# ScalarE takes some k and v norms, the pieces get a new order, and 35 one-column copies go into the lead

## The chip, the cores and the metric

The kernel runs on one core of one Trainium2 chip. The metric is device time in microseconds; a run counts from the start of the program on the device to its end. Five engines work side by side, each on its own queue in order: TensorE (PE in the profile; its weight loads are PEld), VectorE (DVE), ScalarE (ACT), GpSimd (POOL) and SyncE (SP). They wait for each other on semaphores. PSUM, where TensorE writes, has eight banks here, numbered 0 to 7.

## The reference

Eight batches, eight heads, 576 positions, head size 64, and 32 memory slots; then a feed-forward layer over all 4608 tokens.

```
a    = softmax(phi)                      # over the 32 slots of a head
k_m  = a^T k,  v_m = a^T v               # 32 x 64 for each head
attn = softmax(q k_m^T / 8) v_m
x    = attn, heads side by side          # 4608 x 512
h    = max(x w1, x w2, x w3)             # 4608 x 768
out  = h w_out                           # 4608 x 512
```

## The kernel before, in words

The kernel is a list of small steps (pieces), written out by hand as one string at its end. Each word of it is a piece, a number and a batch: `F8@1` is step 8 of kind F for batch 1. A `!` sets the flag `swap`, which moves the piece's element-wise work to the other engine. `issue` turns a word into instructions, and each engine runs its instructions in the order of the words. Nothing reorders them afterwards. A second string gives the PSUM bank of each piece in turn, so it changes with the order.

The kinds that matter here (lines are those of the kernel before):

- `L0` to `L3`, `J`, `H`, `h`, `Y`: loads of phi, k, v, q (or parts of them) and of the weights, issued by GpSimd (L93, L97, L112, L119, L126), with a cast to bf16 for all but phi. `r` packs k beside a column of ones (L105 on ScalarE with `!`, L107 on GpSimd without).
- `E`: exp of phi (L234, ScalarE). `B`: the sums of k, v and the ones over positions (L256, TensorE, 72 small matmuls; in batches 0 and 1 split into `B0` for k and ones and `B1` for v). `N`: the norm, by the reciprocal of the sum of ones (L276, VectorE), which scales v (L280) and k (L291). `K`: transposes of the result (L306) and their copy out of PSUM, `kvt`. Here too `N0`, `K0` are for k and `N1`, `K1` for v in batches 0 and 1.
- `Q`: q transposed on VectorE (L321), two halves. `S`: scores (L342, TensorE) and their exp on ScalarE (L351). `a`, `s`, `c`, `m`, `X`: transpose, sum, reciprocal, product and transpose back (L401 to L441; `m` on GpSimd, or VectorE with `!`). For batch 0 and half of batch 1 `M`, `R`, `X` do the sum by a matmul with ones and ln and exp on ScalarE.
- `D`: the batch's v sums folded into the weights (L453, TensorE) and copied out (L177 or L181): `D3` gives `wp3`, the others parts of `wp`. `V`: w1 and w2 less w3 (L218), once.
- `F`: the first layer (L504, TensorE), 12 steps for each batch: even ones end in a relu, odd ones in a max on VectorE (L517).
- `t`, `T`: the second layer (L663, L681, L690, L699) with its copy out, and the output's DMA (`g` sends a held output on ScalarE's queue). For batches 2 to 7 the second layer is done instead by seven block products `P0` to `P6` (L615) from sums and differences of blocks: `A` of the activations, `U` of the weights (L540; GpSimd or VectorE by the flag; A with `!` is GpSimd's, U with `!` VectorE's).
- `Z`: matmuls on zeros in the lead; `W`, `O`: w3 transposed, and its product with w_out.

Two k buffers (`ko`), three buffers of packed k and v (`kvr`) and two q buffers take turns, so that a load also waits for the last reader of its buffer.

Of the kernel before, what the change touches and what calls it, by code (L numbers as in the profile page):

```python
# [15 lines left out]
def kernel(  # L16
# [28 lines left out]
    const = ctx.enter_context(tc.tile_pool(name="const", bufs=1))  # L45
# [18 lines left out]
    K1 = NP * NC * KS  # L64
# [65 lines left out]
    warm = const.tile([P, BANK], BF16, name="warm")  # L130
# [7 lines left out]
    for i in range(P // M):  # L138
# [4 lines left out]
    banks = iter(  # L143
        "".join(
            """
            00232204420145545045026402642602460246016042045026402462046064206402640230462064
            20642064206247042074204620460240640420402620420462046240724074204242020460246024
            602345040606426064026406416424126464642460263454342
            """.split()
        )  # L150
    )
# [1 line left out]
    def one_bank():  # L153
        return psum[:, int(next(banks))]
# [58 lines left out]
    def w_diff(n, swap):  # L213

        c, end = [(0, BANK), (BANK, DF), (2 * BANK, 2 * DF), (DF, 2 * BANK)][n]
        while c < end:
            e = min(end, (c // DF + 1) * DF)
            (nc.gpsimd if swap else nc.vector).tensor_tensor(  # L218
                out=w12[:, :, c:e],
                in0=w12[:, :, c:e],  # L220
                in1=w_sb[:, :, 2, c % DF : c % DF + e - c],
                op=ALU.subtract,
            )
            c = e
# [41 lines left out]
                        tile_position=(HP * a, M * j),  # L266
                    )

    def att_kv_norm(b, part=None):

        s = st[b]
        kvp = s["kvp", part]
        if part != 1:
            rden = s["rden"] = work.tile([P, NG], FP32, name="rden")
            s["kvn"] = work.tile([P, 3, P], BF16, name="kvn")
            nc.vector.reciprocal(out=rden, in_=kvp[:, :, 0 if part == 0 else D])  # L276
        rden, kvn = s["rden"], s["kvn"]
        if part != 0:
            v0 = 0 if part == 1 else D + 1
            nc.vector.tensor_tensor(  # L280
                out=kvn[:, 0].rearrange("p (a d) -> p a d", a=NG),
                in0=kvp[:, :, v0 : v0 + D],
                in1=rden.unsqueeze(2).to_broadcast([P, NG, D]),
                op=ALU.mult,
            )
        if part == 1:
            return
        k0 = D if part == 0 else 0
        for g in range(NG):
            kn = kvn[:, 1:3, HP * g : HP * (g + 1)]  # L290
            nc.vector.tensor_scalar_mul(  # L291
                out=kn.rearrange("p h (t d) -> p h t d", t=2),
                in0=kvp[:, g, k0 : k0 + D]
                .rearrange("p (d h) -> p h d", h=2)
                .unsqueeze(2)
                .to_broadcast([P, 2, 2, R]),
                scalar1=rden[:, g : g + 1],
            )

    def att_kv_t(b, swap, part=None):  # L300
# [422 lines left out]
    def ffn2_last(b, c0):  # L723
# [18 lines left out]
        for i, (c, po) in enumerate(zip(cs, pos)):  # L742
# [13 lines left out]
            else:  # L756
                nc.scalar.copy(out=ot[:, c], in_=po)
                nc.scalar.dma_start(out=rows, in_=ot[:, c])

    def issue(b, n, swap):  # L760

        i = int(n[1:]) if len(n) > 1 else None
# [8 lines left out]
            "r": lambda: pack(b, swap),  # L771
            "E": lambda: [att_exp(b, h) for h in (halves if b == 0 else [slice(0, NP)])],
            "B": lambda: att_kv(b, i),
            "N": lambda: att_kv_norm(b, i),
            "K": lambda: att_kv_t(b, swap, i),
            "Q": lambda: att_q(b, i),
            "S": lambda: att_score(b),
# [84 lines left out]
```

## Time and profile before

| | us |
|---|---|
| runs, median of 3 | 161.03 (160.45 to 161.09) |
| the profiled execution's own time | 160.41 |
| its span | 158.6 |
| TensorE busy | 150.2 (95%) |
| VectorE, ScalarE, GpSimd busy | 118.4, 98.4, 105.1 |
| last TensorE piece ends | 155.6 |

The profile is of one execution. A busy time counts what an engine was seen to do, whoever waited for it; idle time of an engine with nothing due costs nothing. The chain of waits goes back from the last instruction to what released it, step by step; what is on it set the end. A row of the cost table reads: line, engine, operation, what it writes and reads, shapes, count, then busy us, the mean of one in ns, and the idle time just before with what ended it. A timeline row reads: start and length in us, engine, line, operation, and the idle time before it, if any, in brackets.

### The profile page before, as it was taken

What the parts mean: (1) busy time and instruction counts of PE and PEld (TensorE: products, weight loads), DVE (VectorE), ACT (ScalarE), POOL (GpSimd) and SP (SyncE); (2) the same over time, 40 slices, a digit from 0 to 9 for tenths busy, and PEclk for the clock granted to TensorE, in tenths of its full rate; (3) what the DMA queues carried; (4) which work ended last, traced back from release to release, by engine and by line L of the source; (5) the groups of instructions that cost most, each with busy time, mean ns of one, the idle gap of its engine ahead of it and who ended that gap; (6) DMA issues with size and microseconds to landing.
All of it is one profiled execution on the core that took longest, in us unless ns stands there. A gap on an engine that the chain in (4) does not pass through costs nothing.

```text
span 158.6 us, 5184 instructions
## 1 busy us (share of the span) xinstructions
PE 150.2 (95%) x2228; PEld 100.0 (63%) x2228; DVE 118.4 (75%) x205; ACT 98.4 (62%) x140; POOL 105.1 (66%) x100
## 2 busy tenths in 40 slices
PE   6996798999899999999999999999999999999992
PEld 2342544673456548646777577787874888888871
DVE  2032802789998997897998889899999868899851
ACT  4206335753787799997787789888976934124210
POOL 7960101993039959949969998999979996910000
PEclk9999999999999999999999999999999999999999
DMA  5999999999999999999999999999803500331544
GB/s 153 162 199 208 206 209 213 281 207 209 205 283 218 301 236 235 315 263 283 276 223 208 230 371 231 250 184 186 262 0 136 198 6 0 132 132 70 198 160 171
DMA packets 22934, 31.78 MB, mean 200 GB/s; under 512 B 1152, under 2 KB 18560, under 8 KB 22912
## 3 DMA queue, kind: packets, MB, share of 16 engines
q0 software_dynamic: 16128, 21.43, 71.3%
q1 hardware_dynamic: 6064, 8.85, 15.6%
q10 hardware_dynamic: 720, 1.18, 2.2%
q8 instruction: 17, 0.28, 0.7%
q14 instruction: 5, 0.04, 0.1%
HBM read 39.32 MB, written 9.44 MB: 307 GB/s over the span
## 4 chain that ended last, share of the span: by engine, by line
PE 66%; DMA 23%; POOL 7%; issue 2%; ACT 1%; POOLq 0%
PE psum L504 24%; PE psum L615 24%; DMA w_sb<-in_moe_w_dram 14%; DMA kvr<-in_v_dram 10%; PE psum L453 4%; PE psum L681 4%; PE psum L256 3%; PE psum L663 2%; POOL ko L97 2%; PE psum L342 2%; POOL qq L112 1%; POOL kvr L97 1%; PE psum L690 1%; PE psum L699 1%; POOL w_sb L119 1%
## 5 line engine op out<-in xcount | busy, mean ns | idle before, releaser
L504 PE MATMUL psum<-hx,wp 128*128 128x288 bf16 x384 | 53.2, 286 | 0.1
L504 PEld LDWEIGHTS <-wp 128*128 128x128 bf16 x384 | 36.4, 98 | 11.7 <-issue 2.1
L517 DVE TENSOR_TENSOR hx<-psum,h 128x576 bf16<-128x576 f32 x48 | 34.9, 750 | 6.1 <-PE psum L504 5.0
L177 ACT CAST wp<-psum 128x1024 bf16<-128x1024 f32 (+1 forms) x29 | 27.5, 993 | 3.6 <-PE psum L453 3.4
L175 ACT ACTIVATE h<-psum 128x576 bf16<-128x576 f32 x34 | 21.5, 656 | 7.5 <-PE psum L504 6.8
L615 PEld LDWEIGHTS <-hx 128*128 128x128 bf16 x192 | 18.4, 98 | 3.5 <-issue 1.1
L164 PE MATMUL psum<-warm 128*128 128x512 bf16 x44 | 12.5, 440 | 1.2 <-DVE warm L131 1.2
L351 ACT ACTIVATE e<-psum 128x576 bf16<-128x576 f32 x16 | 9.5, 649 | 5.9 <-PE psum L342 5.9
L107 POOL COPY kvr<-ko 128x2304 bf16<-128x2304 bf16 x3 | 6.3, 2113 | 10.2 <-DMA ko<-in_k_dram 10.2
L615 PEld LDWEIGHTS <-w_sb 128*128 128x128 bf16 x120 | 11.6, 98 | 2.3 <-issue 0.7
L321 DVE STREAM_TRANSPOSE qT<-qq 128x576 f32<-128x576 f32 x16 | 11.8, 758 | 0.7 <-DMA qq<-in_q_dram 0.7
L629 ACT COPY snap<-psum 128x512 f32<-128x512 f32 x11 | 6.5, 595 | 8.7 <-PE psum L615 8.7
L540 POOL TENSOR_TENSOR w_sb<-hx 128x1024 bf16<-128x1024 bf16 x5 | 10.6, 2123 | 1.5 <-DVE hx L517 1.5
L218 POOL TENSOR_TENSOR w_sb<-w_sb 128x2048 bf16<-128x2048 bf16 x1 | 4.1, 4062 | 10.4 <-PE psum L453 10.4
L179 DVE TENSOR_SCALAR h<-psum 128x576 bf16<-128x576 f32 x14 | 10.3, 746 | 0.7 <-PE psum L504 0.6
L234 ACT ACTIVATE e<-ph 128x1152 bf16<-128x1152 f32 (+1 forms) x9 | 9.6, 1068 | 1.7 <-DMA ph<-in_phi_dram 1.6
L615 PE MATMUL psum<-wo_sb,hx 128*128 128x256 bf16 x72 | 9.8, 273 | 0.0
L615 PE MATMUL psum<-w3T,hx 128*128 128x256 bf16 x72 | 9.8, 273 | 0.0
L540 POOL TENSOR_TENSOR twb<-wp 128x256 bf16<-128x256 bf16 x11 | 7.4, 676 | 3.5 <-ACT wp L177 3.5
L177 ACT COPY ot<-psum 128x512 f32<-128x512 f32 x9 | 5.3, 595 | 7.0 <-PE psum L690 6.1
L647 DVE TENSOR_TENSOR ot<-psum,snap 128x512 f32<-128x512 f32 x12 | 8.2, 684 | 1.8 <-PE psum L615 1.1
L427 POOL TENSOR_TENSOR t<-t,sm 128x1152 bf16<-128x1152 bf16 x4 | 8.5, 2137 | 1.5 <-DVE sm L420 1.0
(104 smaller groups left out, 283.8 us busy)
## 6 DMA issues: line engine op xcount, KB each, us to landing
out_dram<-ot SPq DMA_DIRECT2D x8, 512.0 KB, 5.4
qq<-in_q_dram POOLq DMA_DIRECT2D x7, 576.0 KB, 10.4
ph<-in_phi_dram POOLq DMA_DIRECT2D x7, 576.0 KB, 13.8
ko<-in_k_dram POOLq DMA_DIRECT2D x7, 576.0 KB, 16.9
kvr<-in_v_dram POOLq DMA_DIRECT2D x7, 576.0 KB, 11.3
out_dram<-ot SPq DMA_DIRECT2D x14, 256.0 KB, 2.2
w_sb<-in_moe_w_dram POOLq DMA_DIRECT2D x3, 768.0 KB, 18.2
out_dram<-ot ACTq DMA_DIRECT2D x4, 256.0 KB, 6.7
```

Of the source, the lines that this page charges most:

```text
L164: nc.tensor.matmul(po[:, 0:BANK], lhsT=warm[:, 0:P], rhs=warm, start=True, stop=True)
L175: nc.scalar.activation(out=out_, in_=in_, func=AF.Relu)
L177: nc.scalar.copy(out=out_, in_=in_)
L179: nc.vector.tensor_scalar_max(out=out_, in0=in_, scalar1=0.0)
L234: nc.scalar.activation(out=s["e"][:, js], in_=loaded[b]["ph"][:, js], func=AF.Exp)
L321: nc.vector.transpose(out=s["qT"][:, j].rearrange("p j c r e -> p (j c r e)").bitcast(FP32), in_=loaded[b]["q"][:, j].rearrange("p j c d - ...
L351: nc.scalar.activation(out=e2[:, a].rearrange("p (t r c) -> p t r c", t=2, c=NC), in_=sc[a][:, :, 0:SH].rearrange("p t (c r) -> p t r c", ...
L427: (nc.vector if swap else nc.gpsimd).tensor_tensor(out=t, in0=t, in1=x.to_broadcast(list(t.shape)), op=ALU.mult,)
L504: nc.tensor.matmul(acc[:, h, 0:SH], lhsT=wps[b][:, g, w * DF + ft * P : w * DF + (ft + 1) * P], rhs=attn[:, g, c0 : c0 + SH], start=(g == ...
L517: nc.vector.tensor_tensor(out=hT[:, row(ft), (b % 2) * S : (b % 2 + 1) * S].rearrange("p (h n) -> p h n", h=2), in0=a, in1=s["h1", ft], op ...
L540: eng.tensor_tensor(out=out_, in0=in0, in1=in1, op=op)
L615: nc.tensor.matmul(po[:, q * CH : (q + 1) * CH], lhsT=lhs(k, q), rhs=rhs(k), start=(i < 3 and k == 0 and q == 0), stop=(k == KT and q == 1 ...
```

## The change

`N` gets the flag: with `!` its scaling is done by ScalarE, as two instructions for v and two for k (each with the scale read from `rden`, one value per partition), and by VectorE otherwise, as before. The new order uses it for `N0@1`, `N1@1`, `N@2`, `N@5` and `N@6`. A new piece `p` copies one column of zeros `n` times on ScalarE into a tile that nobody reads; `p8` stands ahead of `E@0` and `p27` behind it. The order of all words behind `F8@0 Y1@0` is new, as are the banks, and the flags of 65 words differ. No word is dropped.

```diff
@@ -143,9 +143,9 @@
     banks = iter(
         "".join(
             """
-            00232204420145545045026402642602460246016042045026402462046064206402640230462064
-            20642064206247042074204620460240640420402620420462046240724074204242020460246024
-            602345040606426064026406416424126464642460263454342
+            00232204420145545045026402642642602460230064065606402640264062046234024604604602
+            46024620462502626024604250264262046262062460256025060252065260620026420642042616
+            241642442462106240620462646426402460426041624631120
             """.split()
         )
     )
@@ -266,7 +266,7 @@
                         tile_position=(HP * a, M * j),
                     )
 
-    def att_kv_norm(b, part=None):
+    def att_kv_norm(b, swap, part=None):
 
         s = st[b]
         kvp = s["kvp", part]
@@ -277,24 +277,33 @@
         rden, kvn = s["rden"], s["kvn"]
         if part != 0:
             v0 = 0 if part == 1 else D + 1
-            nc.vector.tensor_tensor(
-                out=kvn[:, 0].rearrange("p (a d) -> p a d", a=NG),
-                in0=kvp[:, :, v0 : v0 + D],
-                in1=rden.unsqueeze(2).to_broadcast([P, NG, D]),
-                op=ALU.mult,
-            )
+            if swap:
+                for g in range(NG):
+                    nc.scalar.mul(
+                        kvn[:, 0, D * g : D * (g + 1)],
+                        kvp[:, g, v0 : v0 + D],
+                        rden[:, g : g + 1],
+                    )
+            else:
+                nc.vector.tensor_tensor(
+                    out=kvn[:, 0].rearrange("p (a d) -> p a d", a=NG),
+                    in0=kvp[:, :, v0 : v0 + D],
+                    in1=rden.unsqueeze(2).to_broadcast([P, NG, D]),
+                    op=ALU.mult,
+                )
         if part == 1:
             return
         k0 = D if part == 0 else 0
         for g in range(NG):
             kn = kvn[:, 1:3, HP * g : HP * (g + 1)]
-            nc.vector.tensor_scalar_mul(
-                out=kn.rearrange("p h (t d) -> p h t d", t=2),
-                in0=kvp[:, g, k0 : k0 + D]
+            k_ = (
+                kvp[:, g, k0 : k0 + D]
                 .rearrange("p (d h) -> p h d", h=2)
                 .unsqueeze(2)
-                .to_broadcast([P, 2, 2, R]),
-                scalar1=rden[:, g : g + 1],
+                .to_broadcast([P, 2, 2, R])
+            )
+            (nc.scalar.mul if swap else nc.vector.tensor_scalar_mul)(
+                kn.rearrange("p h (t d) -> p h t d", t=2), k_, rden[:, g : g + 1]
             )
 
     def att_kv_t(b, swap, part=None):
@@ -757,6 +766,13 @@
                 nc.scalar.copy(out=ot[:, c], in_=po)
                 nc.scalar.dma_start(out=rows, in_=ot[:, c])
 
+    pads = const.tile([P, 48], BF16, name="pads")
+
+    def pad(n):
+
+        for i in range(n):
+            nc.scalar.copy(out=pads[:, i : i + 1], in_=warm[:, 0:1])
+
     def issue(b, n, swap):
 
         i = int(n[1:]) if len(n) > 1 else None
@@ -771,7 +787,7 @@
             "r": lambda: pack(b, swap),
             "E": lambda: [att_exp(b, h) for h in (halves if b == 0 else [slice(0, NP)])],
             "B": lambda: att_kv(b, i),
-            "N": lambda: att_kv_norm(b, i),
+            "N": lambda: att_kv_norm(b, swap, i),
             "K": lambda: att_kv_t(b, swap, i),
             "Q": lambda: att_q(b, i),
             "S": lambda: att_score(b),
@@ -794,38 +810,39 @@
             "t": lambda: ffn2_begin(b, i),
             "O": lambda: w3_o(i, swap),
             "V": lambda: w_diff(i, swap),
+            "p": lambda: pad(i),
             "Z": lambda: warm_up(i),
         }[n[0]]()
 
 
     for w in """
-        E@0 h2@0 h3@0 h0@0 h1@0 L3@0 Z25@0 B0@0 Y2@0 I@0 N0@0 Z2@0 K0@0! Q0@0 Q1@0 Z9@0 S@0 Z2@0
+        p8@0 E@0 p27@0 h2@0 h3@0 h0@0 h1@0 L3@0 Z25@0 B0@0 Y2@0 I@0 N0@0 Z2@0 K0@0! Q0@0 Q1@0 Z9@0 S@0 Z2@0
         M0@0 M1@0 R0@0 R1@0 W0@0 Y3@0 W1@0 W2@0 Z6@0 O1@0 H3@0 O3@0 O2@0 H1@0 X1@0 B1@0
-        X0@0 N1@0 K1@0 O0@0 Y0@0 D1@0! D0@0! D3@0 F8@0 Y1@0 F10@0! L0@1 L1@1 F6@0 J0@1
-        F0@0! F2@0! D2@0 D4@0 F4@0 F1@0 F3@0 F5@0 F11@0 F7@0 V0@0! E@1 F9@0 B0@1 N0@1
-        t2@0 T2@0! J1@1 Q0@1 L2@1 Q1@1 V2@0 K0@1! t1@0 T1@0 S@1 B1@1 V1@0 V3@0 L3@2 N1@1
-        M1@1 a0@1 s0@1 R1@1 c0@1 K1@1 t3@0 T3@0 D2@1 m0@1! D0@1 X1@1 L1@2 X0@1 D1@1 Q0@2
-        L0@2 t0@0 T0@0! L2@2 L1@3 Q1@2 L0@3 r0@2 F8@1! F4@1 F6@1! F7@1 E@2 F10@1! F2@1
-        F5@1 F0@1 g2@0 B@2 D3@1 L2@3 L3@3 N@2 F9@1 F3@1 K@2! F11@1 g1@0 S@2 F1@1 D1@2!
-        E@3 L1@4 U2@9 D0@2 D3@2 t3@1 T3@1 U0@9 T4@1! L0@4 r0@3 a@2 s@2 c@2 D2@2 B@3 L2@4
-        m@2! U2@2 X@2 F10@2 N@3 F2@2 F11@2 F4@2 F0@2 K@3! L3@4 Q0@3 Q1@3 F6@2 F1@2 F8@2
-        g0@0 F3@2 S@3 F7@2 a@3 F5@2 g3@0 s@3 F9@2 r0@4! E@4 U0@2 c@3 L0@5 U1@9 m@3! t2@1
-        T2@1 X@3 U3@9 D0@3 D3@3 t0@1 T0@1! t1@1 T1@1 L1@5 D2@3 B@4 D1@3! N@4 P1@2! L2@5
-        Q1@4 U1@2 F2@3 F6@3 F3@3 F8@3 L3@5 U3@2 L1@6 U0@3 A0@2! Q0@4 K@4! F4@3! F0@3
-        F9@3 P2@2! A1@2! S@4 A2@2! A3@2! F5@3 E@5 a@4 P4@2 F1@3 r0@5 P0@2 L2@6 F10@3
-        L0@6 s@4 F7@3 c@4 P5@2 m@4 D1@4! D3@4 U1@3 F11@3 P3@2 A0@3! D2@4 B@5 A2@3! N@5
-        D0@4 X@4 T4@3! L1@7 A1@3! F10@4 Q0@5 K@5 F0@4 L3@6 Q1@5 P6@2! S@5 r0@6! F11@4
-        F2@4! F1@4 L0@7 F6@4 F4@4! P1@3 F8@4 a@5 s@5 U2@3 D2@5 D3@5 c@5 P2@3! E@6 m@5
-        A3@3! F5@4 P4@3 F3@4 F9@4 P0@3 D1@5! X@5 B@6 N@6 L2@7 D0@5 P5@3 U3@3 F8@5! F7@4
-        P3@3! r0@7! L3@7 U0@4 F2@5! F10@5 E@7 U0@5 F3@5 Q0@6 A0@4! U1@4 P6@3 F11@5 F4@5
-        Q1@6 F6@5 F9@5 K@6! F0@5 A2@4! U2@4 F5@5 S@6 F7@5 A1@4! a@6 A3@4! B@7 N@7 s@6
-        D3@6 D1@6! P0@4 P1@4 U3@4 K@7! P2@4! F1@5 Q1@7 P4@4 c@6 D0@7 D1@7 D0@6 P3@4 P5@4
-        U0@6 Q0@7 m@6 X@6 D2@6 D3@7 D2@7! A0@5! T4@5 S@7 A1@5! P6@4 F0@6 a@7 s@7 F4@6
-        F10@6 F1@6 c@7 F2@6 U2@5 F6@6 P1@5 F3@6 F7@6 U1@5 P2@5 F8@6 A3@5! F9@6 F11@6
-        P4@5 m@7 X@7 F5@6 P0@5! F6@7 F10@7! A2@5! F2@7 P3@5! F4@7! F0@7 P5@5 F8@7! F1@7
-        F11@7 A0@6! U3@5 P6@5 F5@7 F9@7 U0@7 A1@6 U1@7 A2@6 F3@7 U1@6 P1@6 F7@7 P0@6
-        P2@6! P4@6 U2@6 P1@7 A0@7 A3@6 U3@6 A1@7 U3@7! P2@7! P5@6! P3@6 U2@7! A2@7 A3@7
-        P4@7 P6@6 P0@7! P5@7 P3@7! P6@7 T4@7!
+        X0@0 N1@0 K1@0 O0@0 Y0@0 D1@0! D0@0! D3@0 F8@0 Y1@0 L0@1 L1@1 F10@0! F4@0 F6@0
+        F2@0! D2@0 F0@0 J1@1 D4@0 F3@0 F1@0 F5@0 V1@0! E@1 F9@0 F7@0 F11@0 B0@1 J0@1
+        t3@0 L2@1 t1@0 N0@1! K0@1! Q1@1 T3@0 Q0@1 S@1 V3@0 V0@0 a0@1 U2@9! t2@0 s0@1
+        B1@1 N1@1! M1@1 L3@2 t0@0 c0@1 V2@0 m0@1! L1@2 R1@1 T2@0! X1@1 K1@1! Q0@2 T0@0!
+        X0@1 D1@1! D0@1! U0@9 T1@0 L0@2 D2@1 L2@2 Q1@2 F10@1! F8@1 F6@1 L0@3 F4@1! E@2
+        F9@1 r0@2 D3@1 F7@1 F0@1! F2@1 B@2 N@2! F11@1 E@3 F5@1 F3@1 F1@1 K@2! t1@1 S@2
+        L1@3 t3@1 g2@0 D1@2! L2@3 a@2 U1@9 g3@0 D2@2 s@2 D0@2 g0@0 c@2 L3@3 T3@1 U3@9
+        r0@3 m@2! X@2 T4@1! D3@2 B@3 N@3 T1@1 F0@2! L0@4 Q1@3 F6@2 F2@2 K@3 U2@2 U0@2
+        F8@2 F10@2 Q0@3 D3@3! S@3 F9@2 D1@3! D0@3 a@3 t0@1 s@3 c@3 L1@4 F7@2 g1@0 U1@2
+        L2@4 L3@4 L2@5 F4@2 U0@3 L0@5 r0@4! t2@1 F1@2 L1@5 F11@2 F3@2 E@4 m@3 T0@1! X@3
+        U1@3 F5@2 L3@5 T2@1 F4@3 D2@3 B@4 F6@3 N@4 F2@3! F0@3 K@4! U3@2 F10@3 A0@2! Q0@4
+        L1@6 P1@2 Q1@4 A1@2! F3@3 S@4 P2@2! F8@3 A2@2! a@4 s@4 P4@2 A3@2! c@4 L0@6 D0@4
+        L2@6 D2@4 D3@4 P0@2! E@5 P5@2! F9@3 F7@3 P3@2 F1@3 m@4 F11@3 F5@3 r0@5! P6@2
+        U3@3 D1@4! B@5 X@4 N@5! P1@3 F8@4! Q1@5 F2@4 Q0@5 A0@3! F0@4 K@5! A1@3! L3@6
+        F10@4 F9@4 F6@4! P2@3 S@5 P4@3 L0@7 r0@6! F4@4! F7@4 A2@3! a@5 T4@3! D3@5 D1@5!
+        s@5 F11@4 c@5 A3@3! L1@7 U2@3 P0@3 F5@4 F3@4 E@6 F1@4 L2@7 P5@3! D0@5 B@6 Q1@6
+        D2@5 m@5 N@6! L3@7 X@5 P3@3! P6@3! F0@5! F10@5 F6@5 Q0@6 F2@5 K@6 F3@5 F8@5!
+        F4@5 F5@5 E@7 P1@4! r0@7! A0@4! U2@4 F7@5 F1@5 U0@4 F9@5 P2@4 A1@4! U1@4 P4@4!
+        U0@5 A2@4! D3@6 B@7 D1@6! A3@4! U2@5 P0@4 N@7 Q0@7 U3@4 F11@5 S@6 Q1@7 A0@5!
+        P5@4 K@7! a@6 P3@4 s@6 S@7 P6@4 D0@7 D1@7! A1@5 U1@5! D0@6 P1@5! c@6 m@6! T4@5!
+        D2@7 A2@5! X@6 D3@7 D2@6 P2@5 P4@5 a@7 A3@5! U0@6 F8@6 F0@6! P0@5 F2@6 U3@5 s@7
+        F4@6! c@7 F9@6 m@7 P5@5 F10@6 F3@6 P3@5 X@7 F6@6 F5@6 F1@6 P6@5 U2@6 F11@6 F0@7
+        F7@6 F1@7 F8@7 A0@6 A1@6 U1@6 F2@7 F10@7 F6@7 A3@6 F3@7 F4@7! P1@6! F9@7 P2@6!
+        U3@6 F5@7 P0@6! A2@6! U0@7 F7@7 P4@6 U1@7 F11@7 P3@6! U3@7 A0@7 P1@7 A1@7 P5@6!
+        P2@7 P4@7 U2@7 P6@6 A2@7 A3@7 P0@7 P5@7 P3@7 P6@7! T4@7
     """.split():
         n, b = w.rstrip("!").split("@")
         issue(int(b), n, w.endswith("!"))
```

## The prediction

> **What bounds it now.** I read the page first (parts 1 and 2), then the chain of waits in order of time, then TensorE's own timeline and its waits, then the timelines of ScalarE, VectorE and GpSimd for prices. The page:
>
> ```profile
> PE 150.2 (95%) x2228; PEld 100.0 (63%) x2228; DVE 118.4 (75%) x205; ACT 98.4 (62%) x140; POOL 105.1 (66%) x100
> PE   6996798999899999999999999999999999999992
> DMA  5999999999999999999999999999803500331544
> ```
>
> TensorE is full from the sixth slice (20 us) on, and the DMA engines are full up to 112 us. So there are two bounds: what TensorE has to do, and when the loads of the first batches land. The chain shows where one hands over to the other:
>
> ```profile
> 8.79 21.43 DMA w_sb<-in_moe_w_dram
> ...
> 34.91 15.17 DMA kvr<-in_v_dram
> 50.08 0.14 issue
> 50.22 0.80 PE psum L256 x72
> ```
>
> Up to 50 us the end hangs on loads (the last is v of batch 2, needed by `B@2`); behind it, but for two ScalarE pieces of 0.5 and 0.65 us, everything is TensorE until 155.6. How full TensorE is between the two, its timeline tells (start, length, what, idle before):
>
> ```profile
> 40.19 0.74 PE L256 MATMUL psum<-kvr,e 64*32 64x64 bf16 x72 [0.57 <-DMA kvr<-in_v_dram]
> ...
> 45.80 4.16 PE L504 MATMUL psum<-hx,wp 128*128 128x288 bf16 x32
> 50.22 0.80 PE L256 MATMUL psum<-kvr,e 64*32 64x130 bf16 x72 [0.26 <-DMA kvr<-in_v_dram]
> 50.80 0.44 PE L453 MATMUL psum<-w3o,kvt 64*32 64x512 bf16 x8
> 51.17 1.15 PE L504 MATMUL psum<-hx,wp 128*128 128x288 bf16 x8
> 52.17 0.33 PE L306 MATMUL psum<-ident,kvn 128*128 128x128 bf16 x3
> 52.34 0.65 PE L504 MATMUL psum<-hx,wp 128*128 128x288 bf16 x4
> 53.06 0.48 PE L342 MATMUL psum<-qT,kvt 32*32 32x288 bf16 x32
> 53.53 0.65 PE L504 MATMUL psum<-hx,wp 128*128 128x288 bf16 x4
> 54.20 0.63 PE L453 MATMUL psum<-w_sb,kvt 64*32 64x512 bf16 x16
> ...
> 59.89 2.38 PE L504 MATMUL psum<-hx,wp 128*128 128x288 bf16 x18
> ```
>
> From the starts in this view each piece has a price when nothing holds it up: F 0.49 us, P 0.87, t 0.87 and the rest of its T 0.90, a full T4 1.95, B 0.59 (B0@1 0.73, B1@1 0.79), S 0.41, K 0.17, a D 0.23. Four F in a row take 1.96, but `F11@1` at 52.34 takes 0.72 and `F1@1` 0.67: there TensorE waits, though the view names nobody. From `D1@0` at 26.25 the priced pieces add up to 125.0 us, so without any loss TensorE would end at 151.2; it ends at 155.6. The loss is 4.4 us: 0.8 for the two v loads, about 2.5 for some 0.1 us at each change between a tiled kind (B, D, S) and a full one, and only about 1 us of true waits, all between 50 and 60 us.
>
> **The change, part by part.** Both orders hold the same TensorE pieces (pads, copies and norms put none on it), so the 125.0 us stay. Only losses can move. The part ahead of 26.25 us has the same pieces in the same order.
>
> *Pads.* The nearest ScalarE rows:
>
> ```profile
> L177 ACT COPY kvt<-psum 128x256 bf16<-128x256 bf16 x2 | 0.8, 376 | 5.9 <-PE psum L306 5.9
> L312 ACT ACTIVATE kvtn<-psum 128x128 bf16<-128x128 bf16 x1 | 0.3, 278 | 1.0 <-DVE kvt L181 1.0
> ```
>
> 128 columns less save 98 ns, so one column takes about 0.18 us (nearest end), 0.28 at the most. ScalarE idles from 2.02 (table load) to 3.62 and from 5.09 to 10.94: 7.45 us, or 0.21 for each of 35. At 0.18 they take 6.3 and cost nothing. At 0.28 the copy of `K0@0!` would come 2.3 us late; what hides that is TensorE's wait for weights (O1 begins at 19.64 with wo), and some 0.6 us would remain. I take 0. That they move the ends of ScalarE's instruction blocks: the instruction queue with 5 packets (0.04 MB, 8 KB each) fetches at 46.5, 57.9, 67.5, 112.8 and 127.1 us, and at none of them does any engine's idle time lack a releaser. So 0, either way.
>
> *Norms on ScalarE* (N0@1, N1@1, N@2, N@5, N@6). VectorE pays 0.29 + 2 x 0.34, in fact 0.29 + 0.61 us, since they overlap; it loses 3.6 us of work in all. ScalarE gets 16 small instructions; from the rows 0.23 for 64 columns and 0.28 for 128. No row has a scale read from a tile, so it is bounded by nothing and by as much again: 0.9 us for a whole N with overlap, up to 2.0; I take 1.1. Behind it on ScalarE wait the copies and exps; TensorE's K waits for it. At `K@2!` four F (1.96 us) lie between B and K, against 1.3 us before, so 1.1 is covered, 2.0 just not. At `K0@1!` the cover is about 0.6 us (VectorE's reciprocal at 36.5, t1@0 ends at 37.1) and two instructions take 0.5: K at 37.2 to 37.3, as now (37.20).
>
> The Trainium skill, "ScalarE: Activation LUTs", What ACT_TABLE_LOAD costs, says that each operand read through a pointer adds about 93 ns, and its Rules for kernel authors put multiplications on VectorE. By its figures a whole N would take about 1.15 us (an estimate from that page) against VectorE's 0.90; the sum would stay as it is with the cover of `K@2!`. No run here shows it yet.
>
> *Loads up to batch 2.* The load records say when each load landed: v1 39.9, q2 42.7, k2 45.4, ph2 47.0, v2 49.8. They run one behind the other (2.9 us for a k, q or v, 1.6 for a phi). The new order puts the same bytes ahead of v1 and v2, and GpSimd reaches them sooner (V1, 2 us, stands in the place of V0, 4.06). So `B1@1` still starts at 40.2. From there to `B@2` the new order has 9.9 us of pieces instead of 9.5; with 0.3 of switches it comes at 50.4, when v2 is there. Now 50.22: later by 0.2, with 0.4 more done. Gain 0.2.
>
> *Batch 2.* From `B@2` to the first F of batch 2 there are now 8.8 us of pieces, which take 9.67 (50.22 to 59.89). The new order has 10.2 (t1@1, t3@1, T3@1, T4@1, T1@1 stand there as filler). The path that must fit: S@2 ends at 54.4, two exps to 55.7, VectorE a 0.77, s 1.35, c 0.38, m 1.36 (`m@2!` is VectorE's in both orders), X 0.78, with overlaps to 60.2. TensorE needs it at 50.4 + 10.2 + 0.4 switches = 61.0. It fits, so the 0.5 us of waits in this stretch vanish. By then the new order has done 1.8 us more than the old one at 59.89: 61.0 against 61.7. Gain so far 0.7.
>
> *After that* TensorE never waits now, so nothing more can be won, and three loads come close. q3: k3, v3 and q3 move behind ph3, and three outputs (g2, g3, g0) now run between 55 and 60 (two did before, 0.6 us each); q3 lands at about 62.0 instead of 61.2. Its two transposes (0.7 each, one copy between) end at 64.0, S@3 could start at 63.7: 0.3 lost, between 0 and 0.9. `r0@5!` goes from GpSimd to ScalarE (2.1 us) and k5 goes behind v5: the rival below, 0 here. A0@2 to A3@2 on GpSimd (2.13 each) from 72.4 end before P4@2 and P3@2 need them, by 0.7 and 0.9. Fewer switches or free banks may give back 0.3. Net gain 0.7, with -0.2 and +1.3 as ends.
>
> The profiled execution took 160.41 us around its span of 158.6, and lies at the lower end of the runs shown (160.45 to 161.09, median 161.03). 160.41 - 0.7 = 159.7; on the median 160.3. A measurement of this kernel can tell about 0.5% (0.8 us) from no change, so the forecast lies just inside that bound.
>
> **Rivals.**
> 1. *Everything fits* (q3 in time, switches fewer): gain 1.3, 159.7. For it: VectorE has 3.6 us less. Against: v1 still sets 40.2, and the switches are in both.
> 2. *The gain is given back in small waits* (q3 0.9 late, N at its upper price at `K@2!`): 161.0, no change.
> 3. *Slower: ScalarE stands still for k5.* ScalarE works in order; `r0@5!` holds it until k5 has landed, with P6@2's copy, D1@4's copy and N@5 queued behind it, and B@5 needs its result. Now k5 lands at 81.4 and GpSimd does it in time. In the new order ph5, v5 and k5 are the same bytes with k5 last, and before the last of them landed at 84.3. Then the pack ends at 86.7 and B@5 comes at 87.0. From 84.6 on each us of k5 is a us of the whole: if the outputs of T0@1 and T2@1, now at 71 to 73, push k5 by 2 us, the end is 1.3 us after today's: 162.3. In the old trace the same three loads took 10.3 us instead of 7.4 because of outputs, so a push of this size is in reach.
> 4. *It doesn't do what it says*: pads reach `K0@0!` at 0.28 each: +0.6, 161.6.
>
> **How the numbers follow.** Forecast 0.42, rival 1 0.20, rival 2 0.15, rival 3 0.18, rival 4 0.05. Faster by over 0.5% (under 160.2): rival 1 and about half of the forecast, 0.42. Slower (over 161.8): rival 3 and a little of 4 and 2, 0.23. Within: 0.35. The range reaches from rival 1 less half the spread of the runs (0.3) and its 0.5 of unknown switches, 158.9, to just past rival 3, 162.4.
>
> **What would show it.** Right: B1@1 at 40.2, B@2 at 50.4, the first F of batch 2 at 61.0, TensorE ending about 0.7 us ahead; pads of 0.2 us or less, no engine idle for them; ScalarE's kvn instructions of 0.25 to 0.4 us. Wrong: a wait of TensorE over 0.5 us anywhere behind 61 us, first at S@3 (VectorE's qT idle for q) or B@5 (ScalarE's kvr copy idle for k); or v1 or v2 landing at other times than 39.9 and 49.8.

## The result, and the profile after

The changed kernel takes 166.01 us (165.45 to 166.84, 6 runs), the kernel before 160.78 (160.45 to 161.09, 6 runs): ratio 1.0327, 95% interval 1.0305 to 1.0349. It is slower by 5.2 us; the forecast was 160.3 with a range to 162.4. The profiled execution took 165.8 us around a span of 164.0. In the runs below, a ratio leaves out executions over 1.5% above the fastest of their kernel (one each in e4 and e13, two in e12), which the median keeps.

The same three lines of the page:

```profile
PE 150.3 (92%) x2217; PEld 100.0 (61%) x2228; DVE 121.1 (74%) x197; ACT 105.6 (64%) x189; POOL 100.1 (61%) x98
PE   7987789999999985998999999999999899979992
DMA  5999999999999998899999999999606103302454
```

TensorE is busy as long as before (150.3 against 150.2 us) in a longer span: only waits were added. They sit in the slices below 9 of the PE row behind the lead, each 4.1 us long: the 8 and 5 from 57 to 66 us, the 8 at 74, the 8 at 127 and the 7 at 144. TensorE's timeline (start, length, what, idle before) puts numbers to them:

```profile
40.12 0.75 PE L256 MATMUL psum<-kvr,e 64*32 64x64 bf16 x72 [0.30 <-DMA kvr<-in_v_dram]
...
50.32 0.80 PE L256 MATMUL psum<-kvr,e 64*32 64x130 bf16 x72
...
62.99 0.65 PE L513 MATMUL psum<-hx,wp 128*128 128x288 bf16 x4 [1.84 <-ACT ot L177]
...
76.39 0.81 PE L256 MATMUL psum<-kvr,e 64*32 64x130 bf16 x72 [0.64 <-ACT e L234]
...
129.95 1.15 PE L513 MATMUL psum<-hx,wp 128*128 128x288 bf16 x8 [0.77 <-ACT wp L177]
...
146.75 0.65 PE L513 MATMUL psum<-hx,wp 128*128 128x288 bf16 x4 [1.10 <-DVE h L179]
```

The first two rows are `B1@1` and `B@2`, where the prediction put them. The third is `F0@2!`: its first weights were loaded at 60.79 (61.0 forecast), but it started at 62.99. Measured piece by piece against the prices of the prediction, the loss is 2.3 us by the end of `B@3`, in the old order 2.6. Behind it the new order loses 2.5 at `F0@2!` and `F6@2`, 1.1 at `F4@3` and `D2@3`, 1.0 ahead of `F8@6` and 1.2 at `F5@7`; in all 10.2 against 4.4.

The waits of the engines (who waited for what: us in total, times, longest) name the first cause:

```profile
POOL twb L549 <- ACT wp L177: 6.8, 1, 6.8
ACT ot L177 <- DMA out_dram<-ot: 3.3, 3, 2.4
ACT kvr L105 <- DMA ko<-in_k_dram: 2.3, 2, 2.1
PE psum L513 <- ACT ot L177: 1.8, 1, 1.8
```

The second row has no counterpart before: ScalarE's copies of outputs wait for output DMAs. In ScalarE's timeline, and under it GpSimd's:

```profile
56.02 2.84 ACT L177 CAST wp<-psum 128x1024 bf16<-128x1024 f32 x3
61.27 0.59 ACT L177 COPY ot<-psum 128x512 f32<-128x512 f32 x1 [2.41 <-DMA out_dram<-ot]
62.35 0.59 ACT L177 COPY ot<-psum 128x512 f32<-128x512 f32 x1 [0.50 <-DMA out_dram<-ot]
62.84 1.02 ACT L177 CAST wp<-psum 128x1024 bf16<-128x1024 f32 x1
64.25 0.59 ACT L177 COPY ot<-psum 128x512 f32<-128x512 f32 x1 [0.40 <-DMA out_dram<-ot]
...
73.16 2.12 ACT L105 COPY kvr<-ko 128x2304 bf16<-128x2304 bf16 x1 [2.11 <-DMA ko<-in_k_dram]
```

```profile
56.36 0.78 POOL L93 DMA_DIRECT2D ph<-in_phi_dram  x1
63.94 1.29 POOL L549 TENSOR_TENSOR twb<-wp 128x256 bf16<-128x256 bf16 x2 [6.79 <-ACT wp L177]
65.19 0.76 POOL L97 DMA_DIRECT2D ko<-in_k_dram  x1
```

In the old order the same copies followed the casts at once, and k4 was issued far earlier. The rows of before, the third from its page (how long such an output takes from issue to landing):

```profile
58.47 1.13 ACT L177 COPY ot<-psum 128x512 f32<-128x512 f32 x2
49.55 0.76 POOL L97 DMA_DIRECT2D ko<-in_k_dram  x1
out_dram<-ot ACTq DMA_DIRECT2D x4, 256.0 KB, 6.7
```

`opool` has four buffers, and batch 0's four outputs stay in them until `g2`, `g3`, `g0` and `g1` have sent them. In the new order `T3@1`, `T4@1!` and `T1@1` copy out soon behind the sends of g2, g3 and g0 (issued from 54.77 to 56.8), and each needs the buffer of one of these. In the changed kernel such an output takes a median of 6.9 us from issue to landing: g2 lands at 61.19, g3 at 62.28, g0 at 64.18, and each of the three copies starts 0.1 us behind one of them. So ScalarE, in order, stands still from 58.86 to 61.27; `T4@1!` keeps its PSUM bank, which `F0@2!` needs; and `wp3` of `D3@2`, next on ScalarE, is late for GpSimd's `U2@2`, with k4's issue behind it (65.2; 49.5 before). k4 lands at 73.1 (65.2 before), and the pack `r0@4!` holds ScalarE for 2.1 us more.

The waits near the end are of another kind. VectorE's rows, and then GpSimd's of the same stretches:

```profile
123.05 1.33 DVE L420 TENSOR_REDUCE sm<-t 128x36 f32<-128x1152 bf16 x1
124.30 1.28 DVE L549 TENSOR_TENSOR w_sb<-w_sb,hx 128x1024 bf16<-128x1024 bf16 x1
126.70 2.37 DVE L436 TENSOR_TENSOR t<-t,sm 128x1152 bf16<-128x1152 bf16 x1
142.87 2.49 DVE L549 TENSOR_TENSOR w_sb<-hx,w_sb 128x1024 bf16<-128x1024 bf16 x1
```

```profile
122.91 2.13 POOL L549 TENSOR_TENSOR hx<-hx 128x1024 bf16<-128x1024 bf16 x1
125.73 2.13 POOL L549 TENSOR_TENSOR w_sb<-hx,w_sb 128x1024 bf16<-128x1024 bf16 x1 [0.69 <-DVE w_sb L549]
127.81 1.79 POOL L549 TENSOR_TENSOR twb<-wp 128x256 bf16<-128x256 bf16 x1
142.26 2.56 POOL L549 TENSOR_TENSOR hx<-hx 128x1024 bf16<-128x1024 bf16 x1 [3.86 <-DVE w_sb L549]
```

Nobody is named as waiting here; the instructions themselves are long. `A1@5` takes 1.28 and `A3@6` 2.49 us on VectorE, where such a sum takes 0.69; `m@6!` takes 2.37 instead of 1.36. Each ends 0.5 to 1.2 us after the GpSimd instruction that was under way when it began (125.04, 127.86, 144.82). The other way round, GpSimd's `twb` took 1.79 instead of 0.67 beside `m@6!`. In the old order no such sum or product ran beside one of GpSimd's for more than 0.2 us: VectorE's sums lay between 141 and 150 us, behind GpSimd's last, and its products took 1.36. Three rows of before:

```profile
70.08 1.36 DVE L427 TENSOR_TENSOR t<-t,sm 128x1152 bf16<-128x1152 bf16 x1
145.17 0.69 DVE L540 TENSOR_TENSOR w_sb<-hx,w_sb 128x1024 bf16<-128x1024 bf16 x1
138.55 0.67 POOL L540 TENSOR_TENSOR twb<-wp,twb 128x256 bf16<-128x256 bf16 x1
```

In the changed kernel `X@6` is late by it for `F8@6`, and `F4@7!`'s copy for the PSUM bank of `F5@7`. The row of `F8@6` above names a cast of ScalarE, which ended 0.04 us behind `X@6`; its weight load names `X@6` (line 450):

```profile
129.94 0.85 PEld L513 LDWEIGHTS <-wp 128*128 128x128 bf16 x8 [1.05 <-DVE hx L450]
```

### The profile page after: what moved, and what is told of

Same layout as the page of the kernel before. It is cut to its first block, busy times and chain, and to the rows that moved or that the text cites. A ratio compares the mean times of both kernels' runs of the same rounds, so it can differ in the third digit from the quotient of the medians.

```text
span 164.0 us, 5203 instructions
## 1 busy us (share of the span) xinstructions
PE 150.3 (92%) x2217; PEld 100.0 (61%) x2228; DVE 121.1 (74%) x197; ACT 105.6 (64%) x189; POOL 100.1 (61%) x98
## 5 line engine op out<-in xcount | busy, mean ns | idle before, releaser
L175 ACT ACTIVATE h<-psum 128x576 bf16<-128x576 f32 x33 | 20.4, 655 | 7.4 <-PE psum L513 7.2
L179 DVE TENSOR_SCALAR h<-psum 128x576 bf16<-128x576 f32 x15 | 11.3, 751 | 6.4 <-PE psum L513 4.9
L549 POOL TENSOR_TENSOR twb<-wp 128x256 bf16<-128x256 bf16 x12 | 9.5, 799 | 6.8 <-ACT wp L177 6.8
L549 POOL TENSOR_TENSOR hx<-hx 128x1024 bf16<-128x1024 bf16 x5 | 11.1, 2217 | 3.9 <-DVE w_sb L549 3.9
L164 PE MATMUL psum<-warm 128*128 128x512 bf16 x42 | 11.3, 419 | 1.4 <-DVE warm L131 1.2
L549 POOL TENSOR_TENSOR w_sb<-hx 128x1024 bf16<-128x1024 bf16 x4 | 8.5, 2130 | 4.7 <-DVE hx L526 2.4
L638 ACT COPY snap<-psum 128x512 f32<-128x512 f32 x8 | 4.8, 597 | 10.2 <-PE psum L624 10.2
L107 POOL COPY kvr<-ko 128x2304 bf16<-128x2304 bf16 x2 | 4.2, 2102 | 11.0 <-DMA ko<-in_k_dram 11.0
L105 ACT COPY kvr<-ko 128x2304 bf16<-128x2304 bf16 x4 | 8.5, 2119 | 2.3 <-DMA ko<-in_k_dram 2.3
L256 PEld LDWEIGHTS <-e 64*32 64x32 bf16 x720 | 7.1, 89 | 3.5 <-issue 1.1
```

The lines of the kernel that those rows point to most:

```text
L105: nc.scalar.copy(out=out_, in_=in_)
L164: nc.tensor.matmul(po[:, 0:BANK], lhsT=warm[:, 0:P], rhs=warm, start=True, stop=True)
L175: nc.scalar.activation(out=out_, in_=in_, func=AF.Relu)
L179: nc.vector.tensor_scalar_max(out=out_, in0=in_, scalar1=0.0)
L549: eng.tensor_tensor(out=out_, in0=in0, in1=in1, op=op)
```

## The experiments

All changes are made to the changed kernel if not said otherwise. Times are medians; ratios are to the kernel before on the same chip, with 95% intervals.

**e1, room for eight outputs.** A buffer holds two outputs, and the first eight now share in pairs.

```diff
-        ot = opool.tile([P, 2, DM], FP32, name="ot")[:, 0]
+        if len(pairs) % 2 == 0 or len(pairs) > 8:
+            pairs.append(opool.tile([P, 2, DM], FP32, name="ot"))
+            ot = pairs[-1][:, 0]
+        else:
+            pairs.append(None)
+            ot = pairs[-2][:, 1]
```

> The changed kernel, with the eight outputs of batches 0 and 1 put in pairs into the four output buffers (each buffer has room for two), so that no copy of batch 1 has to wait until an output of batch 0 has been sent. Theory 1 (ScalarE stands still for a full set of output buffers): its wait of 2.41 us ahead of T3@1's copy and the two of 0.4 to 0.5 behind it vanish, TensorE's wait of 1.8 us at F0@2 with them; D3@2's wp3 comes 2.4 us earlier, so GpSimd issues k4 at about 62.8 instead of 65.2. Time 162 to 163.5. Theory 2 (the outputs only show up there; the loads and outputs share full DMA queues, and the order of the pieces is what costs): the wait moves to q3 or to the scores of batch 3, time 165.5 to 166.5.

Measured: 163.01 us, ratio 1.0138 (1.0092 to 1.0183), 3.0 us less. ScalarE and TensorE in its trace:

```profile
59.00 1.11 ACT L177 COPY ot<-psum 128x512 f32<-128x512 f32 x2
```

```profile
60.82 0.59 PE L699 MATMUL psum<-wp,hx 128*128 128x512 bf16 x2
61.25 1.63 PE L513 MATMUL psum<-hx,wp 128*128 128x288 bf16 x12
```

The copies follow the casts at once, and twelve matmuls from `F0@2!` on follow `T1@1` without a gap. k4 is issued at 62.35, as theory 1 had it. Theory 2 falls.

**e2, loads of batch 4 ahead of GpSimd's wait.**

```diff
-K@3 U2@2 U0@2 ... c@3 L1@4 F7@2 g1@0 U1@2 L2@4 L3@4 L2@5
+K@3 L1@4 L2@4 L3@4 U2@2 U0@2 ... c@3 F7@2 g1@0 U1@2 L2@5
```

> The changed kernel, with the issues of k4, v4 and q4 ahead of GpSimd's weight differences U2@2 and U0@2 instead of behind them. Theory 1 (ScalarE's pack r0@4! waits 2.1 us for k4 because GpSimd stood 6.8 us in front of k4's issue): k4 is issued near 57 and lands near 67 to 68, the pack waits for nothing, and TensorE's losses at F4@3 and D2@3 (1.1 us over) vanish: 164.6 to 165.2. Theory 2 (k4 is late because the queues are full in any case): k4 lands at 70 or later, 165.7 to 166.3. Theory 3 (the earlier loads delay the outputs for which ScalarE waits): the wait ahead of T3@1's copy grows, 166.5 to 168.

Measured: 166.16 us, ratio 1.0331 (1.0261 to 1.0402). Theory 1 has the mechanism: k4 lands at 68.6, the pack waits for nothing, and the loss at `D2@3` is gone. Theory 3's wait ahead of `T3@1`'s copy did not grow (2.22 us instead of 2.41), though the two behind it did (0.96 and 0.56 instead of 0.50 and 0.40). What took the gain back in the profiled execution is mostly something that no theory had. TensorE's rows:

```profile
63.36 0.65 PE L513 MATMUL psum<-hx,wp 128*128 128x288 bf16 x4 [2.10 <-ACT ot L177]
64.28 2.08 PE L513 MATMUL psum<-hx,wp 128*128 128x288 bf16 x8 [0.27 <-ACT wp L177]
```

Eight such matmuls take 1.14 us in the changed kernel. From 64.0 to 67.5 us TensorE's granted clock was 0.50 instead of 1.00, right behind its wait of 2.1 us, and `F0@2!` to `F10@2` lose 1.7 us more.

**e3, sums back on VectorE.**

```diff
-A2@5! X@6 ... A3@5! U0@6 ... A2@6! U0@7
+X@6 A2@5 ... A3@5 U0@6 ... A2@6 U0@7
```

> The changed kernel with three flags taken back: A2@5 and A3@5 (behind X@6) and A2@6 on VectorE instead of GpSimd, so that VectorE's sums of bf16 tiles and its product m@6 run while GpSimd does nothing. VectorE gets 2.1 us more to do. Theory 1 (VectorE and GpSimd shut each other out while both read such tiles): m@6 takes 1.36 instead of 2.37 us, A1@5 and A3@6 0.69 instead of 1.28 and 2.49, TensorE's waits of 1.0 at F8@6 and 1.1 at F5@7 or P0@6 vanish: 163.6 to 164.2. Theory 2 (these instructions are slow by themselves, or TensorE would have waited anyway): they keep their length, or the added 2.1 us of VectorE show, 165.8 to 167.

Measured: 163.63 us, ratio 1.0165 (1.0114 to 1.0217), 2.4 us less. VectorE has more to do and is done earlier:

```profile
123.35 0.68 DVE L549 TENSOR_TENSOR w_sb<-w_sb,hx 128x1024 bf16<-128x1024 bf16 x1
125.36 1.36 DVE L436 TENSOR_TENSOR t<-t,sm 128x1152 bf16<-128x1152 bf16 x1
141.54 0.69 DVE L549 TENSOR_TENSOR w_sb<-hx,w_sb 128x1024 bf16<-128x1024 bf16 x1
```

The same three instructions have their old lengths, and behind 90 us no piece of TensorE loses more than the 0.36 of a change of kinds. Theory 1 holds.

**e4, both.** The edits of e1 and e3 together.

> Both edits together: eight outputs in the four buffers, and the three sums back on VectorE. If the two causes are separate, the gains add up: 166.0 less 2.5 to 4 less 1.8 to 2.3, so 159.7 to 161.7. If one only hides behind the other, the time is that of the better one alone, 162 to 163.5.

Measured: 160.99 us, ratio 1.0013 (0.9987 to 1.0039). The gains add up (3.0 and 2.4; together 5.0): two separate causes explain the slowdown, within the measurement. Without them the forecast gain still does not show. The following runs start from e4.

**e5, no pads** (`p8@0` and `p27@0` dropped from e4).

> The kernel of e4 without its 35 one-column copies (p8 and p27 dropped). In the trace of the changed kernel they take 0.85 and 2.60 us and end at 7.6 us, with ScalarE then idle for 2.9 us until the copy of K0@0. Theory 1 (they lie in idle time and what they shift costs nothing): the same as e4's 160.99, 160.6 to 161.4. Theory 2 (they shift instruction fetches so that these cost or save a wait): off by 0.5 us or more in either direction, with an idle time of ScalarE that no row explains.

Measured: 164.73 us, ratio 1.0243 (1.0215 to 1.0271). Theory 1 falls: the pads do work. ScalarE's timeline (ACTq: its own queue), and TensorE's:

```profile
55.02 4.35 ACTq L735 DMA_DIRECT2D out_dram<-ot  x1
55.52 0.64 ACT L360 ACTIVATE e<-psum 128x576 bf16<-128x576 f32 x1
59.41 1.01 ACT L177 CAST wp<-psum 128x1024 bf16<-128x1024 f32 x1 [3.25 <-issue]
```

```profile
60.47 1.47 PE L690 MATMUL psum<-wo_sb,hx 128*128 128x512 bf16 x6 [2.88 <-ACT wp L177]
```

"issue" is time for which the profile shows no cause. The issue of g2 took 4.35 us instead of 0.38, and inside it, at 57.84, came an 8 KB packet of the instruction queue. A part of the 3.7 us is again TensorE's clock, which was 0.50 from 61.8 to 65.2, behind the wait of 2.88 us; the page shows it in the sixteenth slice:

```profile
PEclk9999999999999995999999999999999999999999
```

**e6, norms on VectorE** (the five flags on `N` dropped from e4).

> The kernel of e4 with all norms back on VectorE (five flags dropped). Theory 1 (a whole norm takes 1.04 us on ScalarE from first start to last end, 0.9 on VectorE, and other work covers both at K@2, K@5 and K@6): 160.7 to 161.3. Theory 2 (ScalarE's norm is on TensorE's path at K0@1 and in front of the exps of batches 2, 5 and 6): 0.3 to 0.6 faster, 160.4 to 160.7. Theory 3 (VectorE's 3.6 us less are what keeps batches 5 to 7 in time): 161.5 to 162.5, with waits for VectorE behind 110 us.

Measured: 161.66 us, ratio 1.0057 (1.0031 to 1.0084): 0.7 slower than e4, though the intervals touch. Theory 3 has the time but not the place: nothing on TensorE waits for VectorE behind 110 us. The profiled execution (162.69, the slowest of nine) loses 1.25 us at `D2@3`, where TensorE waits for v4, which lands at 75.4 (73.5 in e4), and it was already 0.85 late at `B0@1`. Scaling on ScalarE costs nothing here; whether it gains, this does not settle.

**e7, e4 with the loads of e2.**

> The kernel of e4 with the issues of k4, v4 and q4 ahead of U2@2 and U0@2 as well. In e4 the pack r0@4! still waits 1.28 us for k4, and TensorE loses 0.3 at F4@3 and 0.3 at D2@3. Theory 1 (with the output buffers out of the way nothing is left that an earlier k4 could delay): these two go, 160.4 to 160.7. Theory 2 (as in e2 the earlier loads take bandwidth from outputs or from q3): no change or slower, 160.9 to 161.6.

Measured: 160.63 us, ratio 0.9997 (0.9973 to 1.0022). The time lies in theory 1's range, but from e4 it can't be told, and the trace speaks for theory 2: issued at 57.6 instead of 62.1, k4 still lands at 70.6 (69.9 in e4), the pack waits 1.55 us for it, and `D2@3` loses 0.6. An issue 4.5 us earlier, behind the same loads, did not bring k4 in earlier.

**e8, the kernel before with e1's pairs.**

> The kernel before, with its eight outputs of batches 0 and 1 in pairs in the four buffers. In its trace no copy waits for an output, so all theories expect no change: 160.5 to 161.1. If it gets faster by more than 0.5 us, the pairs do something else than free ScalarE, and the gain of e1 is not only that of the wait.

Measured: 160.62 us, ratio 0.9986 (0.9968 to 1.0005): nothing, as expected. e1's gain is that of the wait.

**e9, k4 ahead of phi 4** (e4 with `L1@4` moved directly ahead of `L0@4`).

> The kernel of e4 with the issue of k4 directly ahead of that of phi of batch 4, as in the kernel before, instead of behind U2@2, U0@2 and phi. In e4 and e7 k4 lands at 69.5 and 70.2, in the kernel before at 64.6, and the pack r0@4! waits for it. Theory 1 (the order in the DMA queue is what makes k4 late): k4 lands at 65 to 66.5, the pack starts at 68.7 right behind the copy ahead of it, the losses at F4@3 and D2@3 (0.6) vanish: 160.2 to 160.6. Theory 2 (the outputs fill the queue in any case): k4 lands at 68 or later, 160.7 to 161.3.

Measured: 160.55 us, ratio 0.9999 (0.9977 to 1.0022). k4 lands at 68.5, later than theory 1 had it and within theory 2. But this is early enough: e4 reached the pack at 68.8, the pack no longer waits, and the loss at `D2@3` is gone, as theory 1 said. In the profiled execution (161.48) a new gap stands at `F9@2`:

```profile
66.33 0.54 PE L513 MATMUL psum<-hx,wp 128*128 128x288 bf16 x3 [0.90 <-issue]
```

TensorE's own 16 KB instruction packet came at 63.98 there, 62.5 in e4. That the packet made the gap is only argued.

**e10, twelve pads** (e4 with `p8@0 E@0 p4@0`).

> The kernel of e4 with 12 pads instead of 35. In all kernels traced so far one 8 KB packet of the instruction queue comes when ScalarE is at its 64th to 66th recorded instruction: at 31.6 to 32.8 us with 35 pads (ScalarE then idles for 2.7 us anyway), at 57.8 us with none. Theory 1 (this fetch stops ScalarE, and the pads put it where that costs nothing): with 12 it comes at the 53rd or 54th of the stream without pads, 49 to 50 us, where norm, copies and exps of batch 2 follow; ScalarE has an idle time of 1 to 4 us there that no row explains, K@2 or S@2 is late, 161.7 to 164. Theory 2 (the 3.25 us in e5 were the DMA issue of the output g2 itself, and the pads only shift it in time): no such idle time at 49 to 53 us, and either 161.0 or again a long issue of g2 at 55 and 164.5.

Measured: 161.01 us, ratio 1.002 (1.0003 to 1.0037). The packet came at 49.3 or 49.9 us (the other is VectorE's), at ScalarE's 66th recorded instruction as foretold, but ScalarE has no unexplained idle time. Theory 1 has the place right and the cost wrong.

**e11, the kernel before with the pads.**

> The kernel before with the same 35 pads in the same two places. There ScalarE's fetch comes at 57.9 us, and no engine's idle time lacks a releaser. Theory 1 (pads cost nothing by themselves: 3.5 us in 7.5 us of idle time; the fetch goes to about 31 us, behind E@1, where ScalarE idles 3.5 us): 160.5 to 161.0. Theory 2 (the pads cost time in the lead, or the fetch at 31 us holds a copy of batch 0): 161.3 to 162.

Measured: 160.61 us, ratio 0.9999 (0.9982 to 1.0016). Pads cost nothing by themselves, and ScalarE's packet moves from 57.9 to 34.3 us.

**e12 and e14, three pads** (e4 with `p3@0 E@0`, the same kernel twice).

> The kernel of e4 with 3 pads. ScalarE's 64th to 66th recorded instruction is then the copy of K@2 and the wait ahead of the exps of batch 2, at 53.6 to 54.5 us, two or three places ahead of the DMA issue of g2. Theory 1 (a fetch is slow, 3 to 4 us, while the loads fill the DMA queue at 54 to 59 us, wherever it falls): ScalarE stands still by 2 to 4 us at 54 to 58, S@2's exps come late, 163.5 to 165. Theory 2 (the fetch alone is short, as with 12 pads, and it is only long where the block ends in the middle of a DMA issue): no idle time over 1 us there, 160.7 to 161.3.

> The kernel of e12 again, for one look at its profile (that of e12 was taken at a granted clock of 0.21 and can't be read). Theory 1 (a fetch is slow wherever it falls under the full queue): ScalarE idle by 1 us or more, with no row that explains it, between 53.6 and 56 us. Theory 2 (long only in a DMA issue): none, and g2's DMA issue takes 0.4 us as in e4. e12 came out at 162.0 in between, so an idle time of some 0.5 to 1 us speaks for a fetch that is slow by the moment.

Measured: e12 162.0 us, ratio 1.0064 (1.004 to 1.0089), between both theories; e14 161.01, a single execution. In e14 the packet comes at 53.4, at the 64th instruction, ScalarE has no unexplained idle time, and g2's issue is short:

```profile
54.85 0.37 ACTq L735 DMA_DIRECT2D out_dram<-ot  x1
```

The 0.8 us by which e12's ratio lies above e4's stay unexplained; e5 lies 3.7 above.

**e13, no pads, norms on VectorE** (e5 and e6 together).

> The kernel of e4 with no pads and with all norms on VectorE, that is the new order alone, with the eight outputs and the three sums on VectorE. ScalarE then has 8 instructions less ahead of 55 us, and its 64th to 66th is behind the issues of g3 and g0, among the three casts of batch 2's folded weights, 57 to 59 us. Theory 1 (slow fetch wherever it falls at 54 to 59 us): ScalarE idle by 2 to 4 us at 57 to 60, T3@1's and T4@1's copies late, 163 to 165. Theory 2 (long only in a DMA issue): 161.0 to 161.8, as e6's 161.66 or a little better.

Measured: 162.0 us, ratio 1.0078 (1.0042 to 1.0113). Its profiled execution took 165.04 us, so only this is read from it: the issues of g2, g3 and g0 take 0.34 to 0.38 us, and the casts and copies from 57.8 to 61.6 follow each other without a gap. The packet came at 60.8, at ScalarE's 70th recorded instruction, behind them all. The time is close to e6's 161.66, which has the pads, so without a DMA issue at the block's end their absence costs little. That is theory 2 by these rows; the time lies 0.2 above its range and 1 below that of theory 1.

**e15, g2 sent one cast later, no pads.**

```diff
-t3@1 g2@0 D1@2! ... U1@9 g3@0
+t3@1 D1@2! ... U1@9 g3@0 g2@0
```

> The kernel of e5 (no pads), with the send of output g2 one cast later, beside g3: the block of ScalarE then ends at the second exp of batch 2 or the cast behind it, not in g2's DMA issue. Theory 1 (slow fetch under the full queue): ScalarE still stands still by about 3 us at 55 to 59 us, 164 to 165. Theory 2 (long only because the block ends in a DMA issue): no long DMA issue, no idle time over 1 us there, 160.7 to 161.5.

Measured: 164.32 us, ratio 1.0233 (1.0166 to 1.03), as theory 1 had the time. But the place speaks for the other:

```profile
55.91 4.00 ACTq L735 DMA_DIRECT2D out_dram<-ot  x2
```

The packet came at 57.9, at the 67th instruction, which here is the issue of g3: this alone took 3.52 us, the one of g2 behind it 0.44. TensorE's clock was again 0.50, from 62.3 to 65.8. So the expectation's own premise failed: the edit put another DMA issue at the block's end. In the two kernels with one there (e5, e15) ScalarE's next cast came over 3 us late; in the others (the kernel before at 57.9 us, e10 at 49, e14 at 53, those with 35 pads at 31.6 to 34.3) the packet met casts, copies, waits or exps, and ScalarE did not stand still without a named cause. That the place decides, and not the load alone, rests on e14 and the kernel before, at 53.4 and 57.9 us. Both long issues ended 1.2 us behind the packet. But both packets came at 57.8 to 57.9 us, though the issues began at 55.0 and 55.9: what held them until then stays open, and why a DMA issue makes the fetch long was not tried.

## Why the prediction was wrong, by its own steps

- **Loads up to batch 2 and Batch 2: right.** `B1@1` at 40.1 (40.2), v2 landed at 50.0 (49.8), `B@2` at 50.3 (50.4), `F0@2!` reached at 60.8 (61.0). The lead over the old order at this point was real. The load times of the prediction are 0.2 to 0.7 us early against the landings that end the waits (v1 40.1, k2 45.9, ph2 47.6, v2 50.1 before); its sum does not hang on that.
- **"After that TensorE never waits now, so nothing more can be won, and three loads come close": the step that failed.** It asked of the filler pieces `T3@1`, `T4@1` and `T1@1` only what they cost TensorE, and of g2, g3 and g0 only what they cost the queue (0.6 us each). The buffer between the two was left out. The page of before had the price: an output of ScalarE's queue took 6.7 us from issue to landing. Issued at 54.8, g2 could not free its buffer before 61.5 by that row, where `T3@1`'s copy was due at 58.9; g3, issued at 56.0, not before 62.7. TensorE's first long wait behind 61 us came so at `F0@2!`, not at `S@3` or `B@5`. It cost 2.5 us there, and through the late k4 part of the 1.1 at 75 us: 3.0 by e1.
- **The flags of A and m: not in the sum.** Only the four sums of batch 2 were priced, each by its own row. With GpSimd and VectorE on such tiles at the same time the prices do not hold: 2.4 us by e3. The Trainium skill, "SBUF — State Buffer", SBUF: two separate sides, says that VectorE and GpSimd share one pair of ports as an exclusive lock, held for a whole instruction, and that a VectorE operation with two SBUF inputs takes it too. The trace agrees: `A3@6` ended 0.54 us after GpSimd's sum, and the reduce at 123.05, with one input, kept its 1.33. It was a rule that spoke against this change, and the prediction did not look for it. "VectorE has 3.6 us less" failed with it: its busy time rose from 118.4 to 121.1 us, and the three long instructions are 3.4 us of that.
- **Rival 3: right in mechanism, wrong in place.** At `r0@5!` ScalarE waited 0.2 us for k5; at `r0@4!` 2.1 for k4, by the same in-order queue. That k4's issue had moved behind `U2@2`, and so behind GpSimd's wait for ScalarE, was not followed.
- **Pads: cost right, purpose wrong.** They take 0.85 and 2.60 us, 0.10 each rather than 0.18, and cost nothing (e11). "So 0, either way" for the block ends fails: without the pads the new order loses 3.7 us (e5). The reading that no fetch in the old trace stopped an engine was right; it did not carry over to an order that puts a DMA issue at the block's end.
- **Norms: right.** The rows:

```profile
51.38 0.52 ACT L282 ACTIVATE kvn<-psum,rden 128x64 bf16<-128x64 f32 x2 [0.43 <-DVE rden L276]
51.78 0.63 ACT L305 ACTIVATE kvn<-psum,rden 128x128 bf16<-128x128 f32 x2
```

  A whole norm runs from 51.38 to 52.41: 1.03 us, 1.1 forecast, and `K@2!` follows its four F without a gap. The estimate from the Trainium skill, "ScalarE: Activation LUTs", What ACT_TABLE_LOAD costs (1.15), is 0.12 too long.
- **The gain of 0.7:** not seen even with both causes mended. e4 is ahead by 0.6 us at `B@3` and gives it back from there to the end; at `F4@3` and `D2@3`, where the pack still waits 1.28 us for k4, it loses 0.6, while the old order's pack found k4 landed. That is rival 2's "given back in small waits", with k4 in the place of q3. e7 and e9 mend parts of it and stay level with the kernel before; no version here beats it beyond the measurement.

## What to carry to other kernels

A step moved to a place where its engine is free still needs its buffers: for each output count the copies that may be held, take issue to landing from the page, and see whether the next copy in that ring comes later than that. Before moving element-wise work between VectorE and GpSimd, ask what the other is doing at that time; the price of a row holds only if the two did not meet there. Instructions that seem to do nothing may set where an instruction block ends (argued here from e5, e13, e14 and e15, not shown to the end): when a stream gets longer or shorter, look at what stands at the new end, above all a DMA issue on the critical engine. And before a lost microsecond is put down to a wait, read TensorE's clock in the stretch behind it.

## What the runs showed of the hardware

- VectorE's sum of two bf16 tiles takes 0.69 us alone and up to 2.49 beside a GpSimd sum; GpSimd's 2.13 becomes 2.56, a short one's 0.67 becomes 1.79.
- ScalarE's instruction packets of 8 KB came (told from the others by their places) at its 64th to 70th recorded instruction and, in the kernel before, again at its 193rd. The Trainium skill, "Runtime: NRT & Kernel Launch", Instruction fetch mechanics, has the fetch run ahead of the engine, so that crossing a block is mostly hidden. Most block ends here agree; the two at a DMA issue of ScalarE cost 3.3 and 3.1 us of its time.
- TensorE's granted clock fell to 0.50 for 3.4 us in the profiled executions of e2, e5, e13 and e15, each time 0.7 to 1.3 us behind a TensorE wait of 1.9 to 2.9 us. At half the clock 3.4 us hold 1.7 us less of work. Behind the waits of 1.84 us (changed kernel) and 2.15 us (e3) it stayed at 1.00, and in the other kernels whose profile is read here, without a TensorE wait over 1.2 us behind 20 us, too. So a wait of this length can cost more than itself; what decides whether it does is not shown.
- Copies of one column follow each other every 0.09 us on ScalarE, though one takes 0.19 by its row.
